# Paired tokens on a partition and 64-row products in a fused retention and mixer kernel

## The chip, the cores and the metric

The kernel runs on one core of one Trainium2 chip. The metric is the device time of one execution in microseconds. The time of the kernel before is 236.0 us, the median of two runs (235.78 and 236.22).

## The reference

Two layers follow each other. The first is a decaying linear attention (retention) for 4 batches, 8 heads, 768 tokens and head dimension 64; the second is a mixer with a low-rank mixing over tokens and an MLP over channels.

```python
gamma = 1.0 - 2.0 ** (-5.0 - np.arange(H))
for t in range(S):
    state = gamma * state + einsum('bhd,bhe->bhde', k[:, :, t], v[:, :, t])
    y[:, :, t] = scale * einsum('bhd,bhde->bhe', q[:, :, t], state)
x = y.transpose(0, 2, 1, 3).reshape(B, S, H * D)          # (4, 768, 512)
h = x.transpose(0, 2, 1) @ U @ V                          # rank 32, over tokens
u = x + h.transpose(0, 2, 1)
out = u + np.maximum(u @ w_ch1, 0.0) @ w_ch2              # 512 -> 2048 -> 512
```

## The kernel before

Tokens are cut into six chunks of 128 per batch, one token to a partition. The decay is folded into k and q: `ret_k` and `ret_q` (L247, L253) multiply them on GpSimd with powers of gamma, which gives `kd` and `qd` in bf16, and `ret_v` (L259) casts v on ScalarE. Both are transposed, so that two heads of 64 channels fill the 128 partitions: on TensorE for batches 0 and 1 (`ret_Tx`, `ret_T`), by DMA for batches 2 and 3 (`ret_T_dma`). For each chunk there are four groups of products on TensorE.

- S (`ret_S`, L308): eight products of k and q, one a head, each over 64 rows, into the two PSUM banks `SA` and `SB`. VectorE multiplies them with the causal mask into `a` (`ret_mask`, L321).
- The part inside a chunk (`ret_O`, L338): eight products of `a` and `vb`, 128 rows, 64 columns.
- The read of the state (`ret_O`, L334): four products of `qT` and the state of the chunks before, 128 columns, two heads at a time. The state is block-diagonal.
- The update of the state (`ret_sum`, L354): four products of `kd` and `vb`, added up in the bank `ST`. `ret_state` (L365) copies it out on VectorE, with a mask (`bmask4`) that keeps the diagonal blocks.

ScalarE copies the result to `xs`. Then the mixer's token part (`mix_P`, `mix_x`, `mix_h`, `mix_u`) gives `uT`, the first MLP product (`mlp1`, 384 columns of moving data) gives `gT` after a ReLU, and the second (`mlp2`, 512 columns) is added to x and stored.

The order is written out by hand, and each engine takes its instructions in that order. The head treats batch 0 alone: loads run on SyncE's queue (SP) in the order k, q per chunk with v three chunks later (`LAG`), TensorE does idle products in between (`run_idle`), and the loads of the weights on GpSimd's queue are held back by a copy that reads a chunk of v (L506). After that, each batch is a list of slots: 32 of `mlp1` (four products each) and 48 of `mlp2` (two products each). `weave` puts the next batch's attention between the slots. `ret_side` says where: `at[c]` is the slot of a chunk's transposes, `gaps` those of S and O after it, and `lead` how long ahead `ret_in` scales the inputs. Batch 1 lies in `mlp2` of batch 0; batches 2 and 3 begin in the `mlp1` of the batch before. The loads of batch 1 start at slot 14 (`gate`, L139). `evict` chooses between ScalarE and VectorE for a copy by a small running estimate (`Balance`).

Of the kernel before, what the change touches and what calls it, by code (L numbers as in the profile page):

```python
# [12 lines left out]
ALU = mybir.AluOpType  # L13
# [34 lines left out]
def kernel(  # L48
# [31 lines left out]
    rin = ctx.enter_context(tc.tile_pool(name="rin", bufs=6))  # L80
# [6 lines left out]

    n_bank = [0]
# [5 lines left out]
    TP, SA, SB, OB, ST = 3, 4, 5, 6, 7  # L94
# [41 lines left out]
    def load_one(t, b, c, src, nm):  # L136
        n = rin.tile([P, H, D], fp32, tag=nm, name=f"{nm}_{b}_{c}")
        if (b, c) == gate:
            nc.scalar.activation(n[:, 0, :1], lsc, AF.Copy)  # L139
        nc.sync.dma_start(out=n, in_=src[b, :, ts(c, P), :].rearrange("h p d -> p h d"))  # L140
        t[nm, c] = n

    def load_chunk(b, c):
        t = {}
        for src, nm in ((k, "k_n"), (q, "q_n"), (v, "v_n")):
            load_one(t, b, c, src, nm)
        staged[b, c] = (t["q_n", c], t["k_n", c], t["v_n", c])
# [22 lines left out]
    LAG = 3  # L170
    t0 = {}
    for c in range(NCK + LAG):
        if c < NCK:
            load_one(t0, 0, c, k, "k_n")
            load_one(t0, 0, c, q, "q_n")
        if c == 1:
            nc.sync.dma_start(out=Vf, in_=moe_V)
        if c >= LAG:
            load_one(t0, 0, c - LAG, v, "v_n")
    for c in range(NCK):  # L180
        staged[0, c] = (t0["q_n", c], t0["k_n", c], t0["v_n", c])
    nc.sync.dma_start(out=Uf, in_=moe_U.rearrange("(j p) r -> p j r", p=P))
# [5 lines left out]
    def run_idle(n):  # L188
        w = bank(0)
        for _ in range(n):  # L190
            matmul(w, idle[:, :P], idle, DM, start=True, stop=True)
# [5 lines left out]
    nc.gpsimd.iota(tglob, pattern=[[P, NCK]], base=0, channel_multiplier=1,  # L197
# [3 lines left out]
                   allow_small_or_imprecise_dtypes=True)  # L201
    lgam = consts.tile([P, H], fp32)
# [11 lines left out]
    srange = tglob[:, 0:1]  # L214
    ident = consts.tile([P, P], bf16)
    nc.vector.tensor_scalar(ident, jmat, srange, None, op0=ALU.is_equal)
    mask = consts.tile([P, P], bf16)
    nc.vector.tensor_scalar(mask, jmat, srange, None, op0=ALU.is_ge)
    sge = consts.tile([P, 1], fp32)
    nc.vector.tensor_scalar(sge, srange, 64.0, None, op0=ALU.is_ge)  # L220
    bmask = consts.tile([P, P], bf16)
    nc.vector.tensor_scalar(bmask, jmat, 64.0, sge, op0=ALU.is_ge, op1=ALU.is_equal)
    mask4 = mask[:, :].unsqueeze(1).to_broadcast([P, NP, P])
    bmask4 = bmask[:, :].unsqueeze(1).to_broadcast([P, NP, P])
# [4 lines left out]
    rep = consts.tile([RK, NG, RK], bf16)  # L229

    def cast_v():
        nc.vector.tensor_copy(out=rep, in_=ident[:RK, :RK].unsqueeze(1).to_broadcast([RK, NG, RK]))
        nc.vector.tensor_copy(out=Vs, in_=Vf)

    def spread_v():

        for i, bk in enumerate((1, OB)):
            o = bank(bk)[:, :HS]
            matmul(o, rep.rearrange("r g s -> r (g s)"), Vs[:, ts(i, HS)], HS, start=True, stop=True)
            nc.scalar.activation(Vb[:, ts(i, HS)], o, AF.Copy)  # L240
# [6 lines left out]
    def ret_k(b, c, eng):  # L247
        q_n, k_n, v_n = staged.pop((b, c))
        kd = rmid.tile([P, H, D], bf16, tag="kd", name=f"kd_{b}_{c}", bufs=6)
        eng.tensor_tensor(kd, k_n, Gk[:, c].unsqueeze(2).to_broadcast([P, H, D]), op=ALU.mult)  # L250
        rc[b, c] = dict(kd=kd, q_n=q_n, v_n=v_n)

    def ret_q(b, c, eng):  # L253
        qd = rmid.tile([P, H, D], bf16, tag="qd", name=f"qd_{b}_{c}", bufs=3)
        eng.tensor_tensor(qd, rc[b, c]["q_n"], Gq[:, c].unsqueeze(2).to_broadcast([P, H, D]),  # L255
                          op=ALU.mult)
        rc[b, c]["qd"] = qd

    def ret_v(b, c):  # L259
        vb = rmid.tile([P, H, D], bf16, tag="vb", name=f"vb_{b}_{c}", bufs=6)  # L260
        nc.scalar.activation(vb, rc[b, c]["v_n"], AF.Copy)  # L261
        bal.book("A", 0.63)
        rc[b, c]["vb"] = vb

    def ret_in(b, c):
        ret_k(b, c, nc.gpsimd)
        ret_q(b, c, nc.gpsimd)
        ret_v(b, c)
        if b + 1 < B and not by_dma(b):
            load_chunk(b + 1, c)  # L270
# [4 lines left out]
    def ret_T_dma(b, c):  # L275
        r = rc[b, c]
        qkT = rmid.tile([P, 2, NP, P], bf16, tag="qkT", name=f"qkT_{b}_{c}", bufs=6)
        for i, src in ((0, r["qd"]), (1, r["kd"])):
            nc.sync.dma_start_transpose(out=qkT[:, i], in_=src.rearrange("p h d -> p (h d)"))
            r["qk"[i] + "T"] = qkT[:, i].rearrange("p n t -> p (n t)")  # L280

    def ret_Tx(b, c, who):

        r = rc[b, c]
        if "qkT" not in r:
            r["qkT"] = rmid.tile([P, 2 * DM], bf16, tag="qkT", name=f"qkT_{b}_{c}", bufs=6)
        i = "qk".index(who)
        tp = bank((2, TP)[i], bf16, 2 * DM)[:, :DM]
        for p in range(NP):
            nc.tensor.transpose(tp[:, ts(p, P)], r[who + "d"][:, ds(2 * p, 2)], ident)  # L290
            bal.mm(P)
        r[who + "T"] = r["qkT"][:, ts(i, DM)]
        nc.scalar.activation(r[who + "T"], tp, AF.Copy)  # L293

    def ret_T(b, c):
        if by_dma(b):
            return ret_T_dma(b, c)
        r = rc[b, c]
        tp = bank(TP, bf16, 2 * DM)
        for i, src in ((0, r["qd"]), (1, r["kd"])):  # L300
            for p in range(NP):
                nc.tensor.transpose(tp[:, ds(i * DM + p * P, P)], src[:, ds(2 * p, 2)], ident)  # L302
                bal.mm(P)
        qkT = rmid.tile([P, 2 * DM], bf16, tag="qkT", name=f"qkT_{b}_{c}", bufs=6)
        evict(qkT, tp, 2 * DM, dve_rate=0.5)
        r["qT"], r["kT"] = qkT[:, :DM], qkT[:, DM:]

    def ret_S(b, c, masks=True):  # L308
        r = rc[b, c]
        sa, sb = bank(SA), bank(SB)  # L310
        for p in range(NP):
            for e, sp in ((0, sa), (1, sb)):
                matmul(sp[:, ts(p, P)], r["kT"][ds(D * e, D), ts(p, P)],
                       r["qT"][ds(D * e, D), ts(p, P)], 80, start=True, stop=True)
        r["a"] = rmid.tile([P, 2, NP, P], bf16, tag="a", name=f"a_{b}_{c}", bufs=5)
        r["s"] = (sa, sb)
        if masks:
            ret_mask(b, c, 0)
            ret_mask(b, c, 1)

    def ret_mask(b, c, e):  # L321
        r = rc[b, c]
        nc.vector.tensor_tensor(r["a"][:, e], r["s"][e].rearrange("p (n t) -> p n t", n=NP), mask4,  # L323
                                op=ALU.mult)
        bal.book("V", 0.69)

    def ret_O(b, c, whole=True, bks=(OB,)):
        r = rc[b, c]
        first = c == 0
        o = [bank(bk) for bk in bks]  # L330
        n = NP // len(o)
        if not first:
            for p in range(NP):
                matmul(o[p // n][:, ts(p % n, P)], r["qT"][:, ts(p, P)],  # L334
                       st_p["sb", c - 1][:, ts(p, P)], P, start=(p % n == 0), stop=False,
                       skip_group_check=True)
        for p, e in [(p, e) for i in range(len(o)) for e in (0, 1) for p in range(i * n, i * n + n)]:
            matmul(o[p // n][:, ds(p % n * P + e * D, D)], r["a"][:, e, p], r["vb"][:, 2 * p + e],  # L338
                   D, start=(first and e == 0 and p == 0), stop=True, skip_group_check=True)
        if whole:  # L340
            ret_sum(b, c)
        if len(o) == 1:
            nc.scalar.activation(xs[b][:, c], o[0], AF.Copy)  # L343
            bal.book("A", 0.62)
        else:
            halves(xs[b][:, c], *o)
        if by_dma(b):
            if first:
                xTs[b] = xtp.tile([P, NCB, S], bf16, tag="xT", name=f"xT_{b}")
            nc.sync.dma_start_transpose(out=xTs[b][:, :, ts(c, P)], in_=xs[b][:, c])  # L350
        if whole:
            ret_state(b, c)

    def ret_sum(b, c):  # L354

        r = rc[b, c]
        if c < NCK - 1:
            if c == 0:
                st_p["ps"] = bank(ST)
            for p in range(NP):  # L360
                matmul(st_p["ps"][:, ts(p, P)], r["kd"][:, ds(2 * p, 2)],
                       r["vb"][:, ds(2 * p, 2)], P, start=(c == 0 and p == 0), stop=True,
                       skip_group_check=True)
# [253 lines left out]
```

## Time and profile before

| what | value |
|---|---|
| median of the runs | 236.0 us (235.78 and 236.22) |
| time of the profiled execution | 236.09 us |
| its span, first to last instruction | 234.3 us |
| granted TensorE clock, mean | 1.0 |
| first `mlp1` product (end of the head) | 30.22 us |
| TensorE products | 1747 |
| q, k, v loads | 72 of 256 KB, in pieces of 256 B |
| q, k, v from issue to landing, median | 4.7 to 5.1 us |
| VectorE masks `a` | 48, 685 ns each |
| VectorE state copies | 20, 690 ns each |
| ScalarE copies of v | 24, 625 ns each |
| GpSimd scalings of k and q | 47, 1055 and 1042 ns each |

The span leaves out some time ahead of the first and behind the last instruction, here 236.09 - 234.3 = 1.8 us. A product's duration in the profile includes its way through the array and is longer than the distance to the next product; prices are read from differences of starts. A share of busy time is an average over stages with different limits.

### The profile page before, as it was taken

To read this page: it belongs to the slowest core of one execution; us is meant where nothing else is said; L and a number is where in the kernel's file an instruction comes from. 1 tells how busy PE (TensorE), PEld (TensorE's weight loads), DVE (VectorE), ACT (ScalarE), POOL (GpSimd) and SP (SyncE) were. 2 spreads that over 40 slices of the span, in tenths; PEclk is the share of its full clock that TensorE was granted. 3 is DMA by queue.
4 is the path that set the end of the run, shared out by engine and by line. 5 is a ranking of instruction groups with operands and counts; after the bars stand their busy time and mean duration, and the time that the engine had idled before them with its cause. 6 is when DMAs were issued, how large, how long until landed. Compare 5 with 4: busy or idle time off the path is not lost. (4 is left out here: it accounts for less than half of the span.)

```text
span 234.3 us, 4300 instructions
## 1 busy us (share of the span) xinstructions
PE 226.0 (96%) x1747; PEld 126.7 (54%) x1747; DVE 86.3 (37%) x159; ACT 100.5 (43%) x198; POOL 56.8 (24%) x64
## 2 busy tenths in 40 slices
PE   6897999999999999999999999999999999999995
PEld 2454766655565566656544456565544456654454
DVE  4454730005876111175736312276728110001221
ACT  3466777762234367755210037763220057760000
POOL 2674840025555530350033500800000000000000
PEclk9999999999999999999999999999999999999999
DMA  7999999999999999865699999445441210001212
GB/s 150 218 219 197 162 200 203 193 197 221 202 217 232 222 240 231 228 85 100 143 172 202 250 244 260 91 81 100 100 82 46 89 49 0 0 3 45 80 56 90
DMA packets 103812, 34.56 MB, mean 147 GB/s; under 512 B 95824, under 2 KB 100816, under 8 KB 103792
## 3 DMA queue, kind: packets, MB, share of 16 engines
q1 hardware_dynamic: 99040, 30.09, 62.5%
q0 software_dynamic: 4752, 4.19, 11.4%
q8 instruction: 13, 0.21, 0.4%
q14 instruction: 7, 0.06, 0.1%
HBM read 27.46 MB, written 6.29 MB: 144 GB/s over the span
## 5 line engine op out<-in xcount | busy, mean ns | idle before, releaser
L115 PE MATMUL bk<-w2b,gT 128*128 128x512 bf16 (+2 forms) x416 | 94.9, 363 | 0.0
L115 PE MATMUL bk<-uT,w1b 128*128 128x384 bf16 x512 | 85.6, 326 | 0.0
L120 ACT ACTIVATE gT<-bk 128x384 bf16<-128x384 f32 x114 | 55.9, 490 | 53.2 <-PE bk L115 52.9
L115 PEld LDWEIGHTS <-w1b 128*128 128x128 bf16 x512 | 49.4, 98 | 32.6
L115 PEld LDWEIGHTS <-gT 128*128 128x128 bf16 x416 | 37.6, 98 | 37.3 <-issue 1.5
L250 POOL TENSOR_TENSOR kd<-k_n,Gk 128x512 bf16<-128x512 f32 x24 | 25.3, 1055 | 64.8 <-DMA k_n<-in_k_dram 26.9
L453 DVE TENSOR_TENSOR o_sb<-bk,x 128x512 f32<-128x512 f32 (+2 forms) x26 | 16.9, 649 | 62.4 <-PE bk L115 55.7
L323 DVE TENSOR_TENSOR a<-bk,mask 128x512 bf16<-128x512 f32 x48 | 31.0, 685 | 12.1 <-PE bk L115 12.0
L255 POOL TENSOR_TENSOR qd<-q_n,Gq 128x512 bf16<-128x512 f32 x23 | 24.0, 1042 | 27.8 <-DMA qkT<-qd 23.9
L343 ACT ACTIVATE x<-bk 128x512 bf16<-128x512 f32 x23 | 13.6, 595 | 26.0 <-PE bk L115 26.0
L261 ACT ACTIVATE vb<-v_n 128x512 bf16<-128x512 f32 x24 | 15.0, 625 | 9.3 <-DMA v_n<-in_v_dram 9.3
L115 PEld LDWEIGHTS <-qkT 64*128 64x128 bf16 (+1 forms) x272 | 11.6, 95 | 12.0 <-issue 6.8
L369 DVE TENSOR_TENSOR state<-bk,bmask 128x512 bf16<-128x512 f32 x20 | 13.8, 690 | 10.8 <-PE bk L115 10.8
L122 DVE TENSOR_SCALAR gT<-bk 128x384 bf16<-128x384 f32 x14 | 7.8, 558 | 23.0 <-PE bk L115 22.8
L115 PE MATMUL bk<-idle 128*128 128x512 bf16 x41 | 13.1, 418 | 1.2 <-DVE idle L186 1.2
L124 DVE COPY qkT<-bk 128x1024 bf16<-128x1024 bf16 x5 | 3.5, 691 | 25.6 <-PE bk L302 25.6
L420 DVE TENSOR_TENSOR uT<-bk,xT 128x384 bf16<-128x384 f32 x16 | 8.3, 553 | 6.7 <-PE bk L115 5.8
L115 PE MATMUL bk<-vb,a 128*128 128x64 bf16 x192 | 10.3, 193 | 0.3
L115 PE MATMUL bk<-qkT 64*128 64x128 bf16 x192 | 9.6, 218 | 1.0 <-ACT qkT L293 0.8
L293 ACT ACTIVATE qkT<-bk 128x512 bf16<-128x512 bf16 x12 | 7.2, 596 | 7.6 <-PE bk L290 7.5
L115 PE MATMUL bk<-Vb,P_sb 128*128 128x384 bf16 x32 | 9.5, 326 | 0.0
L115 PE MATMUL bk<-P_sb,Vb 128*128 128x512 bf16 (+2 forms) x26 | 9.4, 363 | 0.0
(59 smaller groups left out, 93.2 us busy)
## 6 DMA issues: line engine op xcount, KB each, us to landing
k_n<-in_k_dram SPq DMA_DIRECT2D x24, 256.0 KB, 4.7
q_n<-in_q_dram SPq DMA_DIRECT2D x24, 256.0 KB, 5.1
v_n<-in_v_dram SPq DMA_DIRECT2D x24, 256.0 KB, 5.0
out_dram<-o_sb SPq DMA_DIRECT2D x23, 256.0 KB, 3.6
w2b<-in_moe_w_ch_dram POOLq DMA_DIRECT2D x4, 512.0 KB, 15.9
w1b<-in_moe_w_ch_dram POOLq DMA_DIRECT2D x3, 512.0 KB, 8.7
w1b<-in_moe_w_ch_dram POOLq DMA_DIRECT2D x2, 256.0 KB, 4.5
qkT<-qd SPq DMA_TRANSPOSE x12, 2.5
```

What stands on the lines that cost most here:

```text
L115: nc.tensor.matmul(o, l, r, **kw)
L120: nc.scalar.activation(o, i, AF.Relu if relu else AF.Copy)
L122: nc.vector.tensor_relu(o, i)
L250: eng.tensor_tensor(kd, k_n, Gk[:, c].unsqueeze(2).to_broadcast([P, H, D]), op=ALU.mult)
L255: eng.tensor_tensor(qd, rc[b, c]["q_n"], Gq[:, c].unsqueeze(2).to_broadcast([P, H, D]), op=ALU.mult)
L261: nc.scalar.activation(vb, rc[b, c]["v_n"], AF.Copy)
L293: nc.scalar.activation(r[who + "T"], tp, AF.Copy)
L323: nc.vector.tensor_tensor(r["a"][:, e], r["s"][e].rearrange("p (n t) -> p n t", n=NP), mask4, op=ALU.mult)
L343: nc.scalar.activation(xs[b][:, c], o[0], AF.Copy)
L369: nc.vector.tensor_tensor(sb, ps.rearrange("p (n t) -> p n t", n=NP), bmask4, op=ALU.mult)
L420: nc.vector.tensor_tensor(uTs[b][:, c, ts(hf, HS)], piece, xTs[b][:, c, ts(hf, HS)], op=ALU.add)
L453: nc.vector.tensor_tensor(o_sb[:, :w], chp.pop((b, j)), xs[b][:, j, ds(lo, w)], op=ALU.add)
```

## The change

Two chunks are loaded as one pair of 256 tokens: partition p gets tokens 2p and 2p + 1, so that one piece of 512 B serves two tokens of a head. A chunk of 128 tokens is then one half of the partitions (index `h`, 64 rows) with an even and an odd token on each (index `e` or `f`), and the even tokens stand first in a chunk everywhere: in the masks, in `Vb`, in `Ub` and in the rows of the output, which is stored in two parts. `g` is the head's place in its pair of heads. All products of a chunk thus run over 64 rows: S in 16 products per call onto quarters of the array (`ret_S`, two calls a pair), the inner part in 16 products with half the rows (`ret_intra`), the state's update and read on quarters (`ret_sum`, `ret_inter`). The state has 64 columns for each head and needs no mask, so it is copied out by either engine. k and q have transposed tiles of their own. The head is written out anew, with k and q of all pairs ahead of v. The slots change from 5 and 4 a chunk to 10 and 8 a pair.

```diff
-        n = rin.tile([P, H, D], fp32, tag=nm, name=f"{nm}_{b}_{c}")
...
-        nc.sync.dma_start(out=n, in_=src[b, :, ts(c, P), :].rearrange("h p d -> p h d"))
+        n = rin.tile([P, H, 2, D], fp32, tag=nm, name=f"{nm}_{b}_{i}")
...
+        nc.sync.dma_start(
+            out=n.rearrange("p h e d -> p h (e d)"),
+            in_=src[b, :, ds(2 * P * i, 2 * P)].rearrange("h (p e) d -> p h (e d)", e=2))
...
+    for what in ("k0", "q0", "k1", "q1", "k2", "q2", "V", "v0", "v1", "v2"):
...
-        for p in range(NP):
-            for e, sp in ((0, sa), (1, sb)):
-                matmul(sp[:, ts(p, P)], r["kT"][ds(D * e, D), ts(p, P)],
-                       r["qT"][ds(D * e, D), ts(p, P)], 80, start=True, stop=True)
+    def ret_S(b, i, f, bks=(SA, SB)):
+        r = rc[b, i]
+        sp = [bank(bk) for bk in bks]
+        for n in range(NP):
+            for g in (0, 1):
+                for h in (0, 1):
+                    matmul(sp[g][ds(D * h, D), ts(n, P)], r["kT"][ds(D * g, D), f, n, ds(D * h, D)],
+                           r["qT"][ds(D * g, D), :, n, ds(D * h, D)], P / 4, start=True, stop=True)
...
+    def ret_intra(b, i, x):
+        r = rc[b, i]
+        for f in (0, 1):
+            for n in range(NP):
+                for h in (0, 1):
+                    g = (h + x) % 2
+                    matmul(r["o"][h][g][:, n], r["a"][ds(D * h, D), f, g, n],
+                           r["vb"][ds(D * h, D), 2 * n + g, f], D / 2,
...
+    def ret_inter(b, i, h):
+        if (i, h) == (0, 0):
+            return
+        r = rc[b, i]
+        for n in range(NP):
+            for g in (0, 1):
+                for e in (0, 1):
+                    matmul(r["o"][h][g][ds(D * e, D), n], r["qT"][ds(D * g, D), e, n, ds(D * h, D)],
+                           st_p["sb", 2 * i + h - 1][ds(D * g, D), n], D / 4, start=False, stop=True,
...
+    def ret_sum(b, i, h):
...
+        for f in (0, 1):
+            for n in range(NP):
+                for g in (0, 1):
+                    matmul(st_p["ps"][ds(D * g, D), n], r["kd"][ds(D * h, D), f, 2 * n + g],
+                           r["vb"][ds(D * h, D), 2 * n + g, f], D / 2,
...
+    def ret_state(b, i, h, eng=None):
+        sb = rst.tile([P, NP, D], bf16, tag="state", name=f"state_{b}_{2 * i + h}", bufs=3)
+        if eng is None:
+            evict(sb, st_p["ps"], DM // 2)
...
+    def ret_O0(b, i):
+        o_banks(b, i)
+        ret_intra(b, i, 0)
+        ret_sum(b, i, 0)
+        ret_state(b, i, 0)
+        ret_inter(b, i, 0)
+
+    def ret_O1(b, i):
+        ret_inter(b, i, 1)
+        ret_intra(b, i, 1)
+        if i < NI - 1:
+            ret_sum(b, i, 1)
+            ret_state(b, i, 1)
+        ret_xs(b, i)
...
-            nc.sync.dma_start(out=out[b, ts(j, P), ds(lo, w)], in_=o_sb[:, :w])
+            for e in (0, 1):
+                nc.sync.dma_start(
+                    out=out[b, ts(j, P), ds(lo, w)].rearrange("(t e) c -> e t c", e=2)[e],
+                    in_=o_sb[ds(D * e, D), :w])
...
+    run_idle(5)
+    ret_S(0, 2, 0)
+    ret_v(0, 0)
+    ret_S(0, 2, 1, S2)
+    ret_mask(0, 2, 0, 0)
+    spread_v()
+    ret_mask(0, 2, 0, 1)
+    nc.gpsimd.tensor_copy(out=Ub[:, 0, :1], in_=t0["v_n", 1][:, 0, 0, :1])
+    load_w1(0, 256)
...
+    ret_v(0, 1)
+    o_banks(0, 0, (2, OB))
+    o_banks(0, 1, (3, SA))
+    o_banks(0, 2, (SB, 0, 1, 2))
+    ret_sum(0, 0, 0)
+    ret_state(0, 0, 0, "A")
+    ret_intra(0, 0, 0)
+    ret_sum(0, 0, 1)
+    ret_state(0, 0, 1, "A")
+    ret_inter(0, 0, 1)
+    ret_mask(0, 2, 1, 0)
+    ret_mask(0, 2, 1, 1)
+    ret_v(0, 2)
+    ret_sum(0, 1, 0)
+    ret_state(0, 1, 0, "A")
...
-            at, lead, gaps, mix_at = [n1 + 7 + 5 * c for c in range(NCK)], 4, (2, 5), n1 + 37
+            at, lead, gaps = [n1 + 5 + 10 * i for i in range(NI)], 5, (3, 6, 9, 13, 15)
+            mix_at = n1 + 41
...
-            at, lead, gaps, mix_at = [10 + 4 * c for c in range(NCK)], 5, (13, 15), n1 + 17
+            at, lead, gaps = [9 + 8 * i for i in range(NI)], 6, (0, 12, 15, 19, 21)
+            mix_at = n1 + 17
```

The five gaps are those of the q transposes, the two S calls with their masks, `ret_O0` and `ret_O1`.

## The prediction

> **What bounds the kernel now.** I read the page first (engine shares, chain, groups), then busy time by stage, then TensorE's timeline of the head and of the stretches where the next batch's attention is woven between the MLP's products, then single timeline windows of some 50 ns.
>
> ```profile
> span 234.3 us, 4300 instructions
> PE 226.0 (96%) x1747; PEld 126.7 (54%) x1747; DVE 86.3 (37%) x159; ACT 100.5 (43%) x198; POOL 56.8 (24%) x64
> ...
> 0.00:30.22 30.22, 25.00 (x272) 14.58 (x273) 15.98 (x45) 17.26 (x33) 18.20 (x27) 1.00 1.11 189
> 30.22:51.02 20.80, 20.80 (x130) 12.52 (x129) 0.89 (x2) 15.91 (x36) 1.42 (x2) 1.00 1.19 202
> 51.02:85.24 34.22, 34.22 (x325) 19.29 (x324) 18.09 (x28) 12.47 (x23) 18.73 (x19) 1.00 1.07 220
> 85.24:136.90 51.66, 51.52 (x383) 27.95 (x380) 23.01 (x39) 19.76 (x39) 13.41 (x13) 1.00 0.93 183
> ```
> The page's first two lines, then four stages (length; busy PE, PEld, DVE, ACT, POOL; granted clock; DMA share; GB/s). From 30.22 us on TensorE is busy without a gap: every ns that attention adds to its queue lengthens the kernel by a ns, and other engines count only where TensorE waits for them. Ahead of 30.22 lies the head, attention of batch 0, where TensorE is padded with idle products and the pace is set by loads and by short chains through DVE and ACT.
>
> ```profile
> 62.13 0.39 PE L115 MATMUL bk<-vb,kd 128*128 128x128 bf16 x4
> 62.35 1.03 PE L115 MATMUL bk<-w2b,gT 128*128 128x512 bf16 x4
> 63.31 0.40 PE L115 MATMUL bk<-qkT 64*128 64x128 bf16 x8
> 63.64 0.61 PE L115 MATMUL bk<-w2b,gT 128*128 128x512 bf16 x2
> ...
> 61.67 0.39 PE L115 MATMUL bk<-state,qkT 128*128 128x128 bf16 x4
> 61.89 0.40 PE L115 MATMUL bk<-vb,a 128*128 128x64 bf16 x8
> ...
> 181.34 3.62 PE L115 MATMUL bk<-w2b,gT 128*128 128x512 bf16 x16
> 184.79 0.38 PE L115 MATMUL bk<-P_sb,Vb 128*128 128x512 bf16 x1
> ...
> 63.31 0.23 PE L115 MATMUL bk<-qkT 64*128 64x128 bf16 x2
> 77.95 0.40 PE L115 MATMUL bk<-x,Ub 128*32 128x512 bf16 x4
> ...
> 12.96 0.40 PE L115 MATMUL bk<-qkT 64*128 64x128 bf16 x8 [0.25 <-ACT qkT L293]
> 13.29 0.49 PE L115 MATMUL bk<-Vs,rep 32*128 32x384 bf16 x2
> ```
> Timeline rows: start, time to the last end, count. Differences of starts are prices. State update (`vb,kd`): 62.35-62.13 = 0.22. State read (`state,qkT`): 0.22. Inside a chunk (`vb,a`): 62.13-61.89 = 0.24 for eight, 0.029 each. A 512-column product: (184.79-181.34)/16 = 0.216. So the four at 62.35 stream until 63.21, S starts at 63.31 and gives way at 63.64: 0.43 for S, of which 0.10 lies ahead of it. In the narrow windows two S products on different row halves start together and end within 0.23 us (in the single records they start 3 ns apart, the next two 56 ns later), and four products on different 32-column strips start together. Eight S products are thus four rounds of 0.056 = 0.22, and the other 0.2 is a drain of 0.10 on entering and 0.10 on leaving the half-array shape. The last two rows show leaving it for another divided shape (32 rows): 0.33 again, so that drain is paid too.
>
> **The change on TensorE, batches 1 to 3.** Per batch of three pairs:
> - Transposes: as many as before; 0.
> - S: 6 calls (f = 0, 1) of 16 products on 64 x 64 quarters. Neighbours lie on four quarters, so four rounds of 0.056 plus two drains: 0.43, 6 calls = 2.6. Before 6 x 0.43; 0.
> - Inside a chunk: 6 calls of 16 products, two row halves: 8 rounds x 0.029 = 0.235. Before 0.24; 0.
> - State update: 5 calls of 16, all on one row half and two column halves: 8 x 0.029 = 0.235; before 0.22; +0.07.
> - State read: 5 calls of 16 on four quarters: 4 x 0.029 = 0.12; before 0.22; -0.5.
> - Drains: `ret_O0` goes full, 64x128, 64x64, full: 3 per pair, 9. `ret_O1` goes full, 64x64, 64x128, 64x64, full: 4, 4 and, without an update in the last pair, 3. 20 x 0.10 = +2.0; before these groups paid none.
> Sum +1.55 a batch, **+4.7 us** in three. The trace shows no product on a quarter, so bounds: if a change between divided shapes cost nothing (8 of the 20 drains), -2.4, leaving +2.3. If update and read rounds took 0.056 as S rounds do (a weight load of 64 columns that doesn't hide under 64 columns of data), 5 x 12 x 0.027 = +1.6 a batch, +9.5 in all; four quarters working only two at a time would cost about as much (S +1.3, read +0.6 a batch: +10.4). I take 0.029 and all drains, since rows show two row halves and four column strips at once, weight loads that run ahead, and the 64x128-to-32x128 drain.
>
> [...]
>
> **Waits in these stretches.** The second S of a pair writes the banks that the first one's masks read: S to its end 0.5, two masks of 0.69 (0.6 apart), so the second bank is free 1.85 after the start; in batch 1 the call comes 0.33 + 3 slots x 0.43 = 1.6 after. A wait of 0.2 if DVE is free, 0.9 if an `o_sb` or `qT` copy stands ahead. It concerns the three pairs of batch 1 and the last pair of batches 2 and 3; elsewhere the slots are MLP1's of 0.65 and three of them suffice. 5 x 0.2 = **+1.0** (0 to 4.5). Queued behind a waiting S are the MLP's own products, so all of it counts. The state copy (256 columns, 0.38 to 0.42, where the masked product took 0.69) has two slots, 0.86 in MLP2, before the read that needs it: 0; if a DVE copy of 0.69 stands ahead of it, 0.5 a call. DVE loses 20 state products of 0.69, which lay off the path: 0. Stores double from 26 to 52 issues, 0.33 each on SP's queue, ahead of the later transposes and loads, which have some 3 us of slack: 0. Batch 1's loads still go at slot 14, 9 us into the MLP; before, the first k, issued at 40.12, reached GpSimd at 51.1 while weights shared the DMA. The weights now start some 5 us earlier (their gate is the second v), so the 11 us shrink; needed after 11.7: 0, and if that cover is gone TensorE waits for GpSimd's 1.04 products.
>
> **The head.** Nine loads of 512 KB in pieces of 512 B replace 18 of 256 KB in pieces of 256 B. Before, they ran at 217 GB/s (window 6 to 16 us); single packets of 512 B took 27.7 ns in this trace (stores) against 18 for 256 B, 1.3 times the rate: some 290 GB/s, 1.8 us a load. k0 at 4.8 (first bytes 1.95, 1.05 to the semaphore as before), q2 at 13.9, v0 16.0, v1 17.8, v2 19.6; the last v before landed near 25.9 (last issue 21.0 plus 4.9). But then chains decide. DVE's half of q2 stands behind two masks: 15.9; its transposes 16.4; ACT copy of 1024 columns (1.02): 17.7; v0's cast 1.04: 18.7; two `Vb` copies: 19.7, which free the state's bank; v1's cast 20.5; then five rounds of update (0.4 to its last write) and ACT copy (0.38 plus 0.1), 0.9 each, with v2's cast between: fifth state 24.8; three x copies on ACT: 26.3. `mix_P` at 26.35; before:
>
> ```profile
> 27.40 0.86 PE L115 MATMUL bk<-x,Ub 128*32 128x256 bf16 x12
> ...
> 30.22 14.95 PE L115 MATMUL bk<-uT,w1b 128*128 128x384 bf16 x91
> ```
> From `mix_P` to the MLP is 2.8 us in both: **-1.0**. Bounds: at an unchanged 217 GB/s v2 lands at 25.2 and it is +0.8; at 350 the chain moves up, -2.0.
>
> **The end.** Each store becomes two of 64 rows; an issue holds SP's queue 0.33 us: **+0.3** on the last (0 if the first half's landing hides it).
>
> Sum: -1.0 + 4.7 + 1.0 + 0.3 = +5.0 on 236.09, the profiled execution's own time (span 234.3 and 1.8 around it); the median of the runs, 236.0, is the same. **241.1 us.**
>
> **Rivals.**
> - B, quarters overlap less (0.056 rounds, or two at a time): +9.5 to +10.4 instead of +4.7: 246. For it: no row shows 64 columns of weights loaded for 64 columns of data. Against: loads run ahead everywhere, and the 0.029 of `vb,a` hides a load of 128. [...]
> - C, no drain between divided shapes: 238.6. Against: 13.29.
> - D, the other side: the head follows its loads. The MLP started 4.3 us after the last v landed; 19.6 + 4.3 = 23.9, -6.3 for the head, 235.7, not slower. It decides if the four updates that don't need v2 are done when v2 lands. For it: before, ACT's `vb` waits for DMA v_n. Against: the first of them waits for the `Vb` copies, at 19.7 by the chain above. With C and 350 GB/s this reaches 231.
> - E, waits by DVE: half of the nine pairs pay 0.9 more, and some copies are late: +3.4, 244.4.
>
> **Chances.** Forecast 0.40 (own range 239.0 to 243.0), B 0.24, C 0.17, D 0.13, E 0.06. Two per cent (240.7), about what a measurement of this kernel tells from no change, cuts my own case in two: slower 0.21 + 0.24 + 0.06 = 0.51; within 0.19 + 0.17 + 0.08 = 0.44; faster 0.05, out of D. The range takes in D's plain value and B's: 235.0 to 247.0.
>
> **What would show it.** Timeline: S call 0.43; `vb,a` groups 0.235 plus 0.10; `state,qkT` 0.12; each shape change 0.10. Starts 0.056 apart in update groups are B; a missing 0.1 is C. The first `uT,w1b` product at 29.2; at 24 it is D. Rows where `bk` waits for DVE `a` above 0.3 are E. I am wrong if the stages from there to the end grow by under 2 or over 8 us.

## Result and the profile after

The changed kernel takes 245.65 us (median of 245.58 and 245.72) against 236.0: a ratio of 1.041, 95% interval 1.036 to 1.045. That is slower, as forecast, and inside the range, but 4.5 us above the 241.1 that was forecast. The profiled execution took 245.58, so 9.5 us have to be found. First the page's span and clock rows (40 slices of 6.1 us, tenths of full clock), then busy time by stage, with the columns as in the prediction:

```profile
span 243.8 us, 5941 instructions
...
PEclk9998599999999999999999999999999999999999
```
```profile
0.00:31.77 31.77, 24.74 (x472) 15.91 (x475) 16.42 (x45) 16.33 (x28) 17.62 (x29) 0.89 1.06 215
31.77:52.57 20.80, 20.80 (x130) 12.52 (x128) 0.90 (x2) 15.90 (x36) 4.04 (x4) 1.00 1.16 235
52.57:89.02 36.45, 35.56 (x534) 19.68 (x540) 17.34 (x27) 11.71 (x21) 18.27 (x18) 1.00 0.90 228
89.02:143.15 54.13, 52.42 (x591) 28.11 (x596) 21.39 (x37) 19.53 (x38) 12.17 (x12) 1.00 0.73 161
143.15:196.15 53.00, 52.26 (x592) 28.09 (x596) 21.69 (x36) 19.17 (x37) 2.04 (x2) 1.00 0.40 76
196.15:239.22 43.07, 42.96 (x263) 24.39 (x263) 4.86 (x8) 15.68 (x32) 0.00 (x0) 1.00 0.18 39
239.22:243.81 4.59, 0.00 (x0) 0.00 (x0) 0.29 (x1) 0.00 (x0) 0.00 (x0) 1.00 0.22 46
```
Two stages of the kernel before that were not shown yet, the stretch in which batch 3 is prepared, and the end:

```profile
136.90:188.46 51.56, 51.42 (x381) 27.98 (x380) 23.14 (x38) 19.40 (x38) 5.08 (x5) 1.00 0.50 112
...
231.53:234.33 2.80, 0.00 (x0) 0.00 (x0) 0.29 (x1) 0.00 (x0) 0.00 (x0) 1.00 0.16 47
```
Stage by stage, after less before: head +1.55 (forecast -1.0); first MLP1 0; the stretches with attention of batches 1, 2 and 3 +2.23, +2.47 and +1.44 (forecast 4.7 + 1.0 in all, measured 6.14); last MLP 0; end +1.8 (forecast +0.3). So the middle came near its price, in part by luck (see "Why the prediction was right or wrong"), and the head and the end missed by 2.5 and 1.5. The `PEclk` row is the first surprise: in slices 4 and 5 the granted clock drops, which it never did before.

Now the prices of the middle. TensorE's timeline of the changed kernel in two stretches:

```profile
102.76 0.42 PE L120 MATMUL bk<-qT,kT 64*64 64x128 bf16 x16
103.11 2.12 PE L120 MATMUL bk<-uT,w1b 128*128 128x384 bf16 x12
...
63.71 0.44 PE L120 MATMUL bk<-vb,kd 64*64 64x64 bf16 x16
64.08 0.62 PE L307 MATMUL bk<-ident,qd 128*128 128x128 bf16 x8
...
65.50 0.32 PE L120 MATMUL bk<-state,qT 64*64 64x64 bf16 x16
65.75 0.41 PE L120 MATMUL bk<-vb,a 64*128 64x64 bf16 x16
```
S holds TensorE 0.35 to the next start, the update 0.37, the read 0.25. In the single records the four quarters of S start 3 ns apart and the rounds of four 56 ns apart (80 from the first to the second); the update's pairs start every 31 or 32 ns (53 from the first to the second), and each change of shape leaves about 0.09 to 0.12 more than the usual distance between starts. That is close to what the forecast assumed: 0.029 a round, and 0.10 for each drain. A single record lasts some 160 ns longer than the distance to the next start, 193 against 32 in the read and 379 against 216 at 512 columns.

The +2.47 holds one wait. First SP's queue (start, time to the last end, count), then VectorE's row, both of the changed kernel:

```profile
123.66 0.58 SPq L145 DMA_DIRECT2D k_n<-in_k_dram  x1
124.29 0.75 SPq L145 DMA_DIRECT2D q_n<-in_q_dram  x1
125.08 1.98 SPq L145 DMA_DIRECT2D v_n<-in_v_dram  x1
127.17 3.90 SPq L417 DMA_TRANSPOSE xT<-x  x2
```
```profile
133.75 1.02 DVE L480 TENSOR_TENSOR uT<-bk,xT 128x384 bf16<-128x384 f32 x2 [1.84 <-DMA out_dram<-o_sb]
```
TensorE stands still for 0.98 us until 134.36, for a bank that this `uT` sum reads. x was ready at 125.31, but its transposes stood behind three loads in SP's queue. The row names a store as releaser; by the last wait in VectorE's own queue (for the second transpose, until 133.6) it is the transpose, and an experiment decides below.

The end: SP's single records show the last four stores issued at 239.00, 239.60, 240.28 and 240.88, held 0.55 to 0.59 each, while VectorE's last sum was ready at 239.54. Before, the last issue came right behind VectorE, at 231.88, and held the queue 0.33. The last store after, then before:

```profile
240.88 0.59 SPq L517 DMA_DIRECT2D out_dram<-o_sb  x1
```
```profile
231.88 0.33 SPq L456 DMA_DIRECT2D out_dram<-o_sb  x1
```

The head's TensorE rows follow the forecast chain to 23.5 us. Then:

```profile
25.41 1.43 PE L120 MATMUL bk<-vb,a 64*128 64x64 bf16 x47 [0.30 <-issue]
...
27.35 1.46 PE L120 MATMUL bk<-ident,x 128*128 128x128 bf16 x12
28.74 0.88 PE L120 MATMUL bk<-x,Ub 128*32 128x256 bf16 x12
...
31.77 0.49 PE L120 MATMUL bk<-uT,w1b 128*128 128x384 bf16 x2
```
Twelve products with `ident` take 1.39 us, 0.116 each; at full clock those of the same size at 64.08 start 0.056 apart. The clock records of the trace say why: half speed from 22.50 to 29.33.

### The profile page after: what moved, and what is told of

The parts are those of the page before. It is cut to its first block, busy times and chain, and to the rows that moved or that the text cites. A ratio compares the mean times of both kernels' runs of the same rounds, so it can differ in the third digit from the quotient of the medians.

```text
span 243.8 us, 5941 instructions
## 1 busy us (share of the span) xinstructions
PE 228.7 (94%) x2573; PEld 128.7 (53%) x2598; DVE 82.9 (34%) x154; ACT 98.3 (40%) x189; POOL 54.1 (22%) x65
## 4 chain that ended last, share of the span: by engine, by line
PE 88%; DMA 3%; ACT 3%; issue 2%; DVE 2%; POOL 1%; SPq 0%; DVEq 0%; ACTq 0%; POOLq 0%
PE bk L120 86%; DMA q_n<-in_q_dram 2%; PE bk L307 2%; DMA out_dram<-o_sb 1%; ACT qT L313 1%; POOL qd L261 1%; ACT state L391 0%; ACT kT L313 0%; DVE o_sb L513 0%; ACT vb L278 0%; ACT Vb L252 0%; ACT Vs L244 0%; DVE a L332 0%; DVE uT L480 0%; DVE qT L315 0%
## 5 line engine op out<-in xcount | busy, mean ns | idle before, releaser
L120 PE MATMUL bk<-w2b,gT 128*128 128x512 bf16 (+2 forms) x394 | 89.8, 362 | 2.5 <-issue 1.9
L125 ACT ACTIVATE state<-bk 128x256 bf16<-128x256 f32 x15 | 5.7, 383 | 27.6 <-PE bk L120 27.6
L278 ACT ACTIVATE vb<-v_n 128x1024 bf16<-128x1024 f32 x12 | 12.6, 1050 | 2.5 <-DMA v_n<-in_v_dram 2.5
L408 DVE CAST x<-bk 128x512 bf16<-128x512 f32 x11 | 7.6, 688 | 11.9 <-PE bk L120 11.7
L120 PEld LDWEIGHTS <-kT 64*64 64x64 bf16 x384 | 6.4, 106 | 8.5 <-issue 7.5
L120 PE MATMUL bk<-vb,kd 64*64 64x64 bf16 x320 | 9.2, 199 | 1.7 <-ACT Vb L252 0.8
L120 PE MATMUL bk<-vb,a 64*128 64x64 bf16 x384 | 10.3, 199 | 0.3 <-issue 0.3
L120 PE MATMUL bk<-qT,kT 64*64 64x128 bf16 x384 | 9.5, 221 | 0.5 <-ACT qT L313 0.4
L120 PEld LDWEIGHTS <-a 64*128 64x128 bf16 x384 | 7.6, 100 | 4.5 <-issue 4.0
L120 PE MATMUL bk<-idle 128*128 128x512 bf16 x26 | 8.7, 466 | 1.2 <-DVE idle L191 1.2
```

Source lines behind the costliest of these rows:

```text
L120: nc.tensor.matmul(o, l, r, **kw)
L125: nc.scalar.activation(o, i, AF.Relu if relu else AF.Copy)
L278: nc.scalar.activation(vb, rc[b, i]["v_n"], AF.Copy)
L408: nc.vector.tensor_copy(out=o[:, :, 1], in_=s[1])
```

## The experiments

The executions of one experiment lie 0.8 to 3.5 us apart here. The profiles show three things that vary in the head: the length of the half-clock stretch, a wait behind a packet of the instruction queue (below), and the time at which the clock first rises (5.43 us in the changed kernel, 5.80 in e5_load, 9.40 to 10.53 in the seven other runs that leave the idle products at the start as they are). The stretches of batches 1 and 3 repeat to 0.01 us where their code is the same, while batch 2's wait for `uT` (above) moves between 0.76 and 1.33. Effects under 1 us are therefore read from the stages of the profile, from the first MLP product of one batch to that of the next: 57.25, 54.13 and 53.00 in the changed kernel (55.03, 51.65 and 51.56 before).

**The price of a shape change (e3_shapes).**

```diff
+        for lo, w in ((0, D), (D, D)) if quarter else ((0, P),):   # ret_intra in ret_O0: on quarters
...
     def ret_O1(b, i):
         ret_inter(b, i, 1)
-        ret_intra(b, i, 1)
         if i < NI - 1:
             ret_sum(b, i, 1)
             ret_state(b, i, 1)
+        ret_intra(b, i, 1)
```


> The changed kernel with fewer changes of the array's shape in batches 1 to 3: the inner part of the first half of a pair in products on quarters (32 instead of 16, each for 64 of the 128 columns of weights), so that it has the shape of the update and read that follow, and in the second half the update directly after the read, ahead of the inner part. Five changes a batch fall away, fifteen in all. Theory drain: each costs 0.10 us, so the time falls by 1.5 us to some 244.1. Rival no drain: a change between two divided shapes is free and the part on quarters costs as much as before, so 245.6; if 64-column weight loads cost more than they hide, it grows by up to 2.4 us (9 calls of 8 rounds by 0.027, and as much again for the second half of the columns).

Measured: 56.75, 54.23, 52.51; the whole 245.75. In batches 1 and 3 that is 0.50 and 0.49 less for five changes fewer: 0.10 each, and twice as many products inside a chunk cost nothing. In batch 2 the wait for the transposes was 1.57 and ate it.

**Both S calls together (e8_smerge).**

```diff
+    def ret_SM(b, i):
+        ret_S(b, i, 0)
+        ret_S(b, i, 1, (OA, OB))
...
-            at, lead, gaps = [9 + 8 * i for i in range(NI)], 6, (0, 12, 15, 19, 21)
+            at, lead, gaps = [5 + 9 * i for i in range(NI)], 5, (0, 14, 20, 22)
```


> In batches 1 to 3 the two S calls of a pair stand in one slot, the second in the banks of O; the slots of the attention parts are set anew for it. Six shape changes fewer per batch, and no S waits for a mask. Theory drain: 0.10 us for each shape change whatever the products (the run with quartered products in the chunk gave 0.49 per batch for five), so -0.6 in each of the three stretches (57.25, 54.13 less its 0.98 wait, 53.00), -1.8 in all. Rival mask waits: if the second S call waits in batch 1, another 0.2 to 0.6 there. Against it: the masks now stand four in a row on VectorE (2.5 us) ahead of the products inside the chunk; if those wait, a stretch gains nothing.

Measured: 57.08, 52.84, 52.76; the whole 245.2. Batches 1 and 3 gain 0.17 and 0.24, not 0.6. In two pairs of batch 1 and one of batch 3 the last quarters start late, by 0.24 and 0.30, and by 0.30, a wait that the changed kernel hasn't got (probably for the banks of O, which are being copied out). With these waits added back the gain would be 0.71 and 0.54, about the 0.6 expected. Batch 2's wait is gone, since with these slots the load is issued sooner.

**Who makes the wait in batch 2 (e4_osb, e5_load).** Two more `o_sb` buffers, and the load moved behind the transposes:

```diff
-            o_sb = outp.tile([P, DM], fp32, tag="o_sb", name=f"o_sb_{b}_{j}_{i}")
+            o_sb = outp.tile([P, DM], fp32, tag="o_sb", name=f"o_sb_{b}_{j}_{i}", bufs=6)
```


> The changed kernel with six output buffers instead of four. Theory buffers: in batch 2 TensorE waits 0.98 us at 133.4 for a copy to uT, which stands behind an output sum on VectorE that waits for the store of the buffer it reuses; that store was held up in SP's queue behind transposes of x. With six buffers the sum doesn't wait: -1.0 us, to some 244.7. Rival: the copy waits for the transposed x itself, which comes late by the same queue; then no change within 0.2 us.

```diff
-                put(side, at[-1] + 1 + 14 * i, lambda i=i: load_pair(b + 1, i))
+                put(side, at[-1] + (1, 22, 29)[i], lambda i=i: load_pair(b + 1, i))
```


> The load of the middle pair of batch 3 is issued after the last ret_O1 of batch 2 instead of seven slots before it; nothing else moves. Theory SP queue: in the changed kernel the transposes of the last two x chunks stood behind that load's three issues on SP's queue (x finished at 125.31, the first transpose was issued at 127.17), so TensorE's wait of 0.98 us at 133.4 for VectorE's uT goes, the stretch from MLP1 of batch 1 to MLP1 of batch 2 falls from 54.13 to about 53.1, the whole by 1.0. Rival transposes themselves: the last pair makes both its x chunks at once, so two transposes in a row, 2.59 us and 1.27 us of SP's queue, and 2.5 us to land are the chain; the wait then shrinks by at most 0.3 and the stretch stays above 53.8. Rival o_sb: the copy order on VectorE makes it, no change.

With the buffers: 54.09, the wait still 0.93 (the whole 246.16). With the load moved, SP's queue and the stage:

```profile
125.83 2.54 SPq L417 DMA_TRANSPOSE xT<-x  x2
128.43 0.58 SPq L145 DMA_DIRECT2D k_n<-in_k_dram  x1
```
```profile
89.48:142.47 52.99, 52.99 (x597) 28.11 (x596) 21.59 (x37) 19.53 (x38) 12.17 (x12) 1.00 0.70 156
```
TensorE is busy for all of it; the stretch is as long as batch 3's, where no loads follow. The loads in SP's queue were the cause, not the store that the row named. The whole: 245.25.

**The end (e2_tail, e6_store1, e11_before64).** The odd rows of the last chunk on ScalarE's queue:

```diff
+                q_out = nc.scalar if e and (b, j) == (B - 1, NCK - 1) else nc.sync
-                nc.sync.dma_start(
+                q_out.dma_start(
```


> The changed kernel, with the second (odd tokens') store of each piece of the last chunk issued by ScalarE's queue instead of SP's. Theory queue: the last copy on VectorE ends at 239.54 of the span, but four issues of about 0.6 us each stand in SP's queue and the last one goes at 240.88; with two queues the last issue goes at about 239.6 and the time falls by 1.0 to 1.4 us, to some 244.4. Rival landing: the last store waits for the DMA engines and not for its issue; then the time stays within 0.3 us of 245.6.

Measured: from the start of the last product to the last end 4.18 instead of 4.82. The two queues issue at the same time, 0.58 behind the last product's start, but the last landing comes 2.1 later, not 1.55 as before the change. So -0.64, half of what was expected. The whole, 245.82, doesn't show it, within the spread of the head.

One DMA for all 128 rows, the destination as two blocks:

```diff
-            for e in (0, 1):
-                nc.sync.dma_start(
-                    out=out[b, ts(j, P), ds(lo, w)].rearrange("(t e) c -> e t c", e=2)[e],
-                    in_=o_sb[ds(D * e, D), :w])
+            nc.sync.dma_start(
+                out=out[b, ts(j, P), ds(lo, w)].rearrange("(t e) c -> e t c", e=2),
+                in_=o_sb[:, :w])
```


> Each output chunk goes out with one DMA over 128 partitions (destination as two blocks of 64 rows) in place of two DMAs of 64 rows. Theory issue time: the last two column groups of the changed kernel need four issues of 0.55 to 0.59 us on SP's queue, spaced 0.6, and the last one starts at 1.88 us after the last product where the kernel before starts its last at 0.58; with one issue per group of 0.33 to 0.6 the time behind the last product falls from 4.8 to 3.0-3.4, the whole by 1.4 to 1.8. Rival landing: the rows of 256 B at a stride of two rows are slow to write; then the last landing stays 3.2 us behind its issue and the gain is under 0.7.

Measured: 283.57, 38 us more. The DMA view of this kernel from 264 us on:

```profile
DMA packets 668, 0.82 MB, mean 43 GB/s; under 512 B 12, under 2 KB 396, under 8 KB 668
```
While these stores run, at 52 GB/s, the share of the 16 DMA engines is about a tenth (11.8% over this window); the loads of the head moved 290 (the changed kernel, 5.43 to 8.85 us). Loads and transposes behind them in SP's queue wait, and TensorE with them (5.9, 4.2 and 8.7 us). Why one DMA onto two blocks of rows is this slow is not shown. Neither theory was tested by this run, so the question went to the kernel before:

```diff
-            nc.sync.dma_start(out=out[b, ts(j, P), ds(lo, w)], in_=o_sb[:, :w])
+            for e in (0, 1):
+                nc.sync.dma_start(out=out[b, ds(j * P + 64 * e, 64), ds(lo, w)],
+                                  in_=o_sb[ds(64 * e, 64), :w])
```


> The kernel before, with each store of 128 rows made two of 64 neighbouring rows; nothing else. Theory issue time: all that the changed kernel lost behind the last product comes from here, so the time behind the last product grows from 3.0 to 4.8 and the whole by 1.8; the stretches stay at 55.03, 51.65, 51.56, or the last two grow by up to 0.5 if SP's transposes come later. Rival: the skip of a row in DRAM costs, not the number of issues; then under 0.5.

Measured: 241.6, ratio 1.022 (1.018 to 1.027). Behind the last product's start 5.10 instead of 3.02: the end's loss comes from splitting each store in two, with no row skipped. What nobody expected is the stretch of batch 2:

```profile
85.27:141.68 56.41, 52.88 (x377) 28.41 (x380) 23.01 (x39) 19.78 (x39) 13.01 (x13) 0.97 0.83 172
```
```profile
131.21 0.33 PE L115 MATMUL bk<-Vb,P_sb 128*128 128x384 bf16 x1 [3.01 <-DVE uT L420]
```
4.8 us more than 51.65. The last two transposes are issued at 126.64 and 127.96 instead of 123.45 and 124.77, TensorE waits 3.01 us for `uT`, and behind that wait the clock is at half from 131.39 to 134.80, which leaves some 1.7 for the clock. This is one execution, the slowest of four (239.45 to 242.95); the wait is not known in the others.

**The head (e1_idle, e7_head, e9_fill, e10_all, e12_quiet).** First, seven idle products of the whole array among the five updates:

```diff
+    run_idle(3, 2)                 # ahead of ret_sum(0, 0, 0)
     ret_intra(0, 0, 0)
+    run_idle(2, SB)
...
+    run_idle(1, SB)                # behind ret_inter(0, 0, 1)
...
+    run_idle(1, SB)                # ahead of ret_sum(0, 2, 0)
```


> The changed kernel with seven idle products of 512 columns put into the gaps of the state chain at the end of the head (three ahead of the first state update, two after the first inner products, one after the first state read, one ahead of the fifth update). Theory clock: the head ends 2.5 us late because the granted clock is 0.5 from 22.5 to 29.3 us of the span; with the gaps filled it stays at 1.0, the first MLP product comes at about 29.3 instead of 31.77 and the time falls by 2 to 2.5 us, to some 243.3. Rival chain: the copies on ScalarE set the pace and the slow clock lies in their shade, or the idle products are too few to hold the clock; then the time stays at 245.6 or grows by up to 0.5.

Measured: 246.78, a loss of 1. The half-clock stretch shrank from 6.83 to 3.41 us, but the first MLP product came at 32.97: a new wait of 1.38 us without a releaser stood in the chain. Then another order of the head, without idle products:

```diff
-    spread_v()
+    copy_v = spread_v()            # second part in bank 3, its copy later
+    copy_v[0]()
...
     ret_sum(0, 0, 0)
     ret_state(0, 0, 0, "A")
+    ret_v(0, 1)
...
-    ret_v(0, 2)
+    ret_v(0, 2, nc.vector)
```


> Only the head is put in another order: the cast of the third v pair on VectorE instead of ScalarE, the first state update no longer behind the second copy of Vb (it goes to bank 3), the second v cast behind the first state copy. Theory ScalarE chain: the fifth state comes about 1.5 us earlier, and TensorE's waits of 0.77, 0.41 and 0.35 us ahead of the first three updates shrink; with the wait shares gone no 3.4 us stretch of the head is under 0.6 busy, the granted clock stays at 1.0, and the first MLP product comes 2 to 4 us earlier than at 31.77. Theory clock alone, set by something else than TensorE's busy share: the half-clock stretch of 6.8 us stays and the gain is at most 1. Rival code: where TensorE waits without a releaser 2.3 us behind a packet of the instruction queue (0.30 in the changed kernel, 1.38, 1.70, 0.75 and 0 in the four runs so far), a quicker chain makes this wait longer, and 1 us of the gain is lost.

Measured: 245.72; from the last S of the head to the first MLP product 12.91 us instead of 13.88. The clock still fell, and that tells busy share from another measure. Stages of 3.41 us: the kernel e1_idle, then e7_head (length, busy PE; the granted clock is third from the end):

```profile
19.70:23.12 3.42, 3.35 (x102) 2.13 (x102) 1.74 (x3) 2.86 (x6) 1.57 (x4) 1.00 1.01 129
23.12:26.53 3.41, 1.82 (x94) 1.42 (x87) 0.69 (x1) 1.45 (x4) 3.41 (x5) 1.00 0.95 138
26.53:29.94 3.41, 3.41 (x98) 3.13 (x97) 1.45 (x3) 1.64 (x4) 1.03 (x2) 0.50 1.23 200
```
```profile
20.04:23.45 3.41, 2.88 (x123) 2.18 (x114) 3.02 (x5) 3.17 (x7) 1.43 (x4) 1.00 1.18 147
23.45:26.87 3.42, 3.10 (x118) 2.65 (x112) 1.11 (x2) 1.88 (x5) 3.42 (x5) 0.50 0.88 121
```
In e7_head TensorE was busy 2.88 of 3.41 us and lost the clock. Counting each product as rows by columns of weights by moving columns, against the whole array at 512 columns in 0.216 us, that stretch used 0.33 of the array; the one of e1_idle that kept the clock used 0.57, the next 0.25. Changes of clock lie 3.41 us apart or a multiple of it (in the changed kernel up at 5.43, down at 22.50, up at 29.33: 17.07 and 6.83, five times and twice 3.41). Over all fourteen profiles the clock fell in the head behind stretches of 0.22 to 0.33 and behind none of 0.38 or more; from half, once it had fallen, it rose behind 0.40 to 0.47 and stayed behind 0.19 to 0.36. In the kernel before the lowest share in its head at full clock is 0.51, from 17.51 to 20.93 us. Busy time does not sort these stretches: the changed kernel kept its clock behind 5.43 to 8.85 us with TensorE busy 1.61 of 3.41 us and a share of 0.41.

More idle products, also ahead of the first transposes:

```diff
-    run_idle(9)
+    run_idle(13)
...
+    run_idle(2, SB)                # five more places among the updates, 12 products in all
```


> Idle products of the whole array are added to the head alone: 13 instead of 9 ahead of the first transposes, and 12 more, two or three at a time, among the five state updates (0.216 us each at full clock, about half of them in waits). Theory array share: in the nine runs so far the granted clock went to a half behind every 3.41 us stretch in which the products filled 0.24 to 0.33 of the array's time (rows by columns by moving columns) and behind none with 0.38 or more, also where TensorE was busy 0.85 of such a stretch; with this fill no stretch is under 0.4, so the clock rises by 5.8 us, stays at 1.0, the last S of the head starts near 17.9, and the first MLP product comes at 29.5 to 30.5 (31.8 to 35.4 in the runs so far); the whole 1.5 to 3 lower, 243 to 244. Theory busy share: the same, since the fill raises both. Rival: the fall has another cause (a fixed time after the start, the DMA load): the half-clock stretch stays, and the added products make the head 1 us longer. Rival code: a wait of up to 1.7 us behind a packet of the instruction queue comes in any case and leaves a gain under 1.

Measured: 247.55, a loss of 2. The clock rose at 4.20, and the last S came at 17.96 as expected, but a wait of 1.68 us without a releaser left its stretch at 0.33, and half clock followed from 28.09 to 31.50. The share of 0.40 that the fill was made for was not reached. The first MLP product: 33.65.

All that helped, together:

```diff
+    # e7_head with idle products (13 ahead, 7 among the updates), e3_shapes, e8_smerge, e2_tail
-            at, lead, gaps = [5 + 9 * i for i in range(NI)], 5, (0, 14, 20, 22)
+            at, lead, gaps = [3 + 10 * i for i in range(NI)], 5, (0, 14, 20, 22)
```


> All that helped, in one: the head in the other order with idle products among its updates; the products inside a chunk on quarters beside the first update, and the second update next to the state read (five shape changes fewer); both S calls of a pair in one slot, with slots set so that the third pair needn't wait for the banks of O; odd stores of the last chunk on ScalarE's queue. By the stretches: 57.25 less 0.5 less 0.2; 54.13 less 1.0 (no wait for the transposes) less 0.5 less 0.5; 53.0 less 0.5 less 0.5; end 4.8 less 0.65; head 31.8 less 2 to 3. Theory of the drains and the clock: 245.6 less 6 to 7 is 238.5 to 240. If terms overlap: 241 to 242. Not under 236: some ten shape changes per batch are left.

Measured: 242.24, ratio 1.025 (1.021 to 1.028). Stages 56.15, 52.79, 51.93, end 4.11: 4.2 us gained against the changed kernel in these four. The clock was full from 6.14 on, lowest share 0.38. Yet the head was 32.74 long:

```profile
25.24 0.32 PE L120 MATMUL bk<-vb,a 64*128 64x64 bf16 x10 [1.06 <-issue]
...
31.98 0.27 PE L120 MATMUL bk<-ident,x 128*128 128x128 bf16 x2 [2.29 <-issue]
```
"issue" is a wait for nothing that the profile shows. In every case it stands in the middle of a group and ends 2.2 to 2.7 us behind the start of a 16 KB packet of the instruction queue (here 22.82 and 29.65). The changed kernel needs 20 such packets in its span where the kernel before needed 13; to 5171 weight loads and products of TensorE (3494 before) that is one for each 259 (269). In the same place of the same head code the wait was 0.30, 1.70, 0.75, 0.83 or 0 us. Counting TensorE's weight loads, products and sequencer records in the order of their starts, the wait stands ahead of number 700 to 705 in all eight profiles that have it, though their heads differ, and the second wait of e10_all ahead of 957, 256 further than its first at 701. A fixed place in the instruction stream speaks for code and against any product's data. The last run kept the weight loads away:

```diff
-    load_w1(512, 512)
...
     mix_P(0, list(range(NCK)), (OB, ST))
+    nc.gpsimd.tensor_copy(out=wgate, in_=Ps[0][:, :1])
+    load_w1(512, 512)
```


> As the run before with all parts together (e10_all), but the weight loads from column 512 of w1 on start only when P_sb of batch 0 is written, near 28.6 us; before, they ran from 21 us on at some 200 GB/s. In e10_all the clock was full through the head, and what made it 32.74 us were two waits of TensorE without a releaser, 1.06 us to 25.24 and 2.29 us to 31.98, each ending 2.3 to 2.4 us behind the start of a 16 KB packet of the instruction queue (22.82 and 29.65). Theory DMA load: the packets are late because the weights fill the DMA queues; without them both waits shrink by over a half, the first MLP product comes near 30, the whole at 239 to 240.5. Theory code by itself: the packet comes when the last block of 256 instructions is used up and takes 2.3 us in any case; both waits stay within 0.5 us, the whole 241.5 to 243. If the first product then waits for w1: up to 1 us more.

Measured: 240.28, ratio 1.016 (1.013 to 1.018), the best version of the change, though not under 236.0. The packet that had come at 29.65 (29.18 to 31.89 in the ten other profiles of the changed head) came at 26.35, and the wait of 2.29 is gone; the earlier packet, at 22.80, kept its wait:

```profile
25.22 0.32 PE L120 MATMUL bk<-vb,a 64*128 64x64 bf16 x10 [1.38 <-issue]
```
The last weights moved until 22.81, and from there to 26.35 no other transfer ran. So the 2.42 us from the packet's start to the next product are not made by weights that move at the same time; whether weights made that packet start late, and what starts a packet, stays open. For the later packet this one pair of profiles speaks for DMA load as the cause.

The profiled execution of e12_quiet took 242.48, the slowest of six and as long as that of e10_all (242.34). Its first MLP product came 1.22 earlier, at 31.52, but two losses stand against that. The clock fell again, behind a stretch with a share of 0.32 and next to no DMA traffic (5 GB/s), so DMA load is not what the clock follows:

```profile
23.32:26.73 3.41, 2.03 (x113) 1.71 (x112) 0.73 (x2) 1.06 (x3) 0.00 (x0) 1.00 0.02 5
26.73:30.14 3.41, 3.41 (x35) 2.49 (x33) 1.15 (x3) 0.96 (x3) 0.55 (x2) 0.50 0.00 0
```
And the weights now move with the loads of batch 1: its first k landed 12.5 us behind its issue instead of 4.2, TensorE waits 0.28 and 0.60 for GpSimd's `kd`, and the first stretch is 57.64 instead of 56.15. That the median is 2 us lower rests on executions without a profile.

## Why the prediction was right or wrong

- **Shape changes**: the mechanism was right, the size 0.3 to 0.5 a batch short. e3_shapes measures 0.10 each. A trace without missing product records (e4_osb) splits batch 3, by distances between starts: S +0.12, read +0.13, update +0.49, inside the chunk +0.08, MLP products behind which a smaller shape begins +0.59: 1.41 against 1.55. That this is so near is luck: the next point's 0.47 is hidden in it, without which it would be 1.88, and in batch 1, where the kernel before had no such waits, the same groups cost +2.05 (S 0.20, read 0.14, update 0.49, inside the chunk 0.63, MLP 0.59). The single records show where: the first round behind a change takes some 0.02 longer than the rounds after it (from start to start 53 ns instead of 31 or 32 in the update and 54 instead of 31 or 32 in the read), and S gives way 0.02 later (0.35 instead of 0.33). Rival B (rounds of 0.056 in the update, or quarters two at a time) and rival C (no drain between divided shapes) fall with the same rows. No row of before had 64 columns of weights for 64 columns of data; after, these rounds of 31 or 32 ns are just that, near the 0.029 of the forecast.
- **"before these groups paid none"**: wrong by a little. The kernel before lost 0.235 twice each in batches 2 and 3, in the middle of `vb,a`, behind masks; the new order has no such waits. That is 0.47 of the 0.8 between batch 1 (+2.23) and batch 3 (+1.44).
- **Waits of the second S, +1.0**: not seen. The S calls of batch 1 cost 2.18 against 2.10 in batch 3, so 0.1 for three pairs. Rival E falls too: no row waits for the masks above 0.3. That the middle measured 6.14 against 5.7 is luck as well, since in place of this 1.0 stands a wait of 1.1 that the forecast put at nothing (next point).
- **"Stores double ... some 3 us of slack: 0"**: the step that failed in the middle. The queue had no such slack at the last transposes of batch 2: 0.98 us in the changed kernel (1.13 by e5_load), 3.0 and a half clock in e11_before64. Each issue was counted, but not against the transposes due just there.
- **The end, +0.3**: mis-sized; +1.8. The split was to cost one more issue of 0.33. But a store of 64 rows holds the queue 0.55 to 0.59, the last four stand in a row, 0.6 apart, and only the last counts: it was issued 1.30 later behind the product, and landed 1.7 later. e11_before64 gives 2.1 with nothing else changed.
- **The head, -1.0**: mis-sized; +1.55. The first loads moved 290 GB/s as forecast (the last v landed at 21.73, not 19.6, and the fifth state came at 25.4, not 24.8), and the chain of copies held to 23.5 us. The step that failed is the unsaid one that TensorE's own products stay at full clock. Without idle products among the updates they fill 0.26 of the array, 6.83 us at half clock follow, and `mix_P` comes at 28.74 instead of 26.35. How much of these 2.4 us is the clock is an estimate: 91 products from 25.41 to 28.74 take 3.33 us at half clock, and 102 of the same kinds in e10_all take 2.29 at full clock, from 25.24 to 27.53; so at least 1.0. No run holds the clock and leaves the order as it was. With the clock held (e10_all) and its two waits behind packets of the instruction queue, 3.35 in all, taken off, the head would be 29.4, near the 29.2 of the forecast, though in another order and with idle products. Rival D fell, since the chain, not the last load, set the pace.

The sign was right for the reason given, the shape changes. The number missed by 4.5, mostly for costs that lie outside TensorE's sum: SP's queue at the end, which e11_before64 and e2_tail show, and the clock in the head, whose fall is shown and whose price is estimated. The wait behind a packet of the instruction queue cost the changed kernel only 0.30, and more in its variants (1.06 and 2.29 in e10_all).

## What to carry to other kernels

Cutting products into halves or quarters of the array is paid at its borders: count the shape changes (0.10 us each here) and put equal shapes together. Where a DMA is split, ask which transfer due soon stands behind the additional issues (a wait of 3.01 us in e11_before64), and look at the end, where nothing hides them (1.8 us here). Where small products stand alone, count how much of the array they fill in each 3.41 us (here 0.33 or less cost the clock), and how many packets of the instruction queue their number needs (20 here, 13 before).

## What the hardware showed unexpectedly

- The granted clock halved though TensorE was busy 0.85 of a stretch of 3.41 us (e7_head, 0.33 of the array filled); in the heads of the fourteen profiles it fell behind 0.22 to 0.33 of the array and behind none of 0.38 or more.
- TensorE waited 0 to 2.3 us at a fixed place of its instruction stream (number 700 to 705), up to twice in a head of some 950 of its records, until 2.2 to 2.7 us behind the start of a packet of the instruction queue; with the weight loads held back (e12_quiet), one of two such waits went.
- At the end of the kernel a store of 64 rows held SP's queue 0.47 to 0.59 us, one of 128 rows 0.33 in the kernel before; one DMA onto two blocks of rows moved 52 GB/s (e6_store1).
- The releaser of a wait can be named wrongly: a store for a transpose, at 133.75.
